# Three groups of 128-token chunks in place of four groups of mixed size, in a fused scan, MoE and Mish-MoE kernel

## The chip, the cores and the metric

The program runs on one core of a Trainium2 chip. The core has five engines with a queue of instructions each: TensorE (PE, matrix multiplies), VectorE (DVE), ScalarE (ACT), GpSimd (POOL) and SyncE (SP); POOL and SP are used here to issue DMAs. Every engine works its queue off in order and waits on semaphores for the others. The metric is the device time of one execution in microseconds (us); lower is better.

## The reference, cut to what matters

Three layers run one after the other on 4 sequences of 768 tokens, 8 heads of 48 (3072 tokens of 384):

```
mag = sqrt(a_re² + a_im²);  a = (a_re, a_im) · min(mag, 0.999) / (mag + 1e-6)
for t in range(768):                       # a complex, diagonal decay
    S = a[t] · S + k[t] v[t]ᵀ              # S is 48 x 48, complex, per head
    y[t] = q[t] · Re(S)
x  = ((y @ w1) * (y @ w2)) @ w3 @ w_out    # first MoE layer, 384 -> 1024 -> 384
h  = x @ w_in                              # second, 384 -> 2048 -> 384
out = (h * tanh(softplus(h))) @ w_out2
```

All values are float32.

## The kernel before, in words

The recurrence is cut into **chunks** of tokens. Inside a chunk the decays are multiplied up from the chunk's middle in both directions, so that scores inside the chunk become a masked matrix product, and between chunks a state `z` is carried. `GROUPS` (L24) lists half chunk lengths: a group holds 8 chunks of twice that length, in token order, and its tables are made together. `[32, 32, 64, 64]` is 16 chunks of 64 tokens, then 16 of 128.

Five kinds of work are written as Python generators ("streams") that yield a weight after each piece:

- `fold_stream` (F): decodes w3 and w_out and multiplies them together (matmuls into `ps_f`, halves `woh` and `wol`).
- `bh_stream(g)`, the **scan** of group g: for all chunks of a group at once, half length + 1 steps, in blocks of 7 steps (`BLK`). `norm` scales the decays of a block (L211 to L237, DVE and ACT in turn); `steps` makes three DVE instructions for each step (L261 `t`, L262 `rv`, L263 `p`), then two wide ones per block (L273 `kt`), which are written to DRAM (`kq_d`) through POOL from one buffer. The last block ends with the group's table `mt`; its last instruction is L299. A group of 32 has 33 steps in 5 blocks, one of 64 has 65 in 10.
- `ch_stream` (CH), the **chunks**: each loads its `tm` from `kq_d`, is transposed on PE (`ps_tr` L372), gives a state update (`ps_u` L380), scores (`ps_a` L415, masked on DVE in two halves, L416) and outputs (`ps_y` L428 and L433); the state goes on through L385, a DMA `ws<-w`, L403 and L404. A chunk can start only when its group's table is there. Its outputs go to DRAM (`xd`); when 512 tokens are there, they come back as one tile of the next layer (`xl`).
- `m1_all` (M), the first MoE layer: 6 tiles of 512 tokens of 8 **M1 steps** each. A step is 27 matmuls (`pa`, `pb`, `acc`, all at L500), with L519 on ACT and `u` L522 on DVE between. Tile 0 also decodes w1 and w2.
- `win_stream`: decodes the weights of the last layer.

`_merge` (L50) draws from several streams so that each advances in proportion to its weight; a stream that yields None waits for another. `until(CH, n)` stops after n chunks, `take(M, w)` after w units of M1 (a step is 6 units). What the merge writes is then ordered once more by the framework's scheduler on each engine, within what dependences allow; the engines' own order is what runs. After the streams, the last layer (`ps_h`, `ps_o`) runs with PE as good as always busy.

Chunks and M1 steps are counted from 0 below; "first table" is the `mt` of group 0, and so on.

Of the kernel before, what the change touches and what calls it, by code (L numbers as in the profile page):

```python
# [20 lines left out]
NT = B * S  # L21
NC = 8

GROUPS = [32, 32, 64, 64]  # L24
TOK0 = [2 * NC * sum(GROUPS[:g]) for g in range(len(GROUPS) + 1)]
assert TOK0[-1] == NT
CMAX = 2 * max(GROUPS)
SIZES = sorted({2 * l for l in GROUPS})
DFF1, DFF2 = 1024, 2048
# [20 lines left out]
def _merge(*gens):  # L50
    live = [[0.0, i, g, w] for i, (g, w) in enumerate(gens)]
    while live:
        live.sort(key=lambda s: (s[0], s[1]))
        s = live[0]
        try:
            w = next(s[2])
            if w is None and len(live) == 1:
                return
            s[0] = live[1][0] + 1e-3 if w is None else s[0] + w / s[3]
        except StopIteration:  # L60
            live.pop(0)
# [3 lines left out]
def kernel(  # L65
# [23 lines left out]
    mul, add, sub = ALU.mult, ALU.add, ALU.subtract  # L89
    NG = len(GROUPS)  # L90

# [5 lines left out]
    sg = const.tile([128, 1], F32, name="sg")  # L97
    n_blk = [-(-(l + 1) // BLK) for l in GROUPS]
    flags = const.tile([128, sum(n_blk) + 1], F32, name="flags")
    wsum = const.tile([128, 64], F32, name="wsum")  # L100
    cb = const.tile([128, 3], F32, name="cb")
    fss = [const.tile([64, 2, D], F32, name=f"fs{z}") for z in range(2)]
    kq_d = [dram.tile([128, l, 2 * D2], F32, name=f"kq_d{g}") for g, l in enumerate(GROUPS)]
    xd = [dram.tile([HD, TT], F32, name=f"xd{i}") for i in range(NTILE)]
# [53 lines left out]
    def fold_stream():  # L158

        wos, *bufs = [wpo.tile([128, 8 * HD], I32, tag=n, name="f" + n) for n in WN]  # L160
        bufs = [(w[:, 0:2048].rearrange("p (n z) -> p n z", z=2), w[:, 2048:3072]) for w in bufs]
        for c in range(3):
            decode(wo[:, c], 1024, wos[:, c * 1024:(c + 1) * 1024], bufs[c][0])
            yield 2.0
        wos = wos.bitcast(F32).rearrange("p (k n) -> p k n", k=8)
        for j in range(8):
            raw, dst = bufs[j % 3]
            f = decode(w3t[:, j], 1024, dst, raw).rearrange("p (k m) -> p k m", k=8)
            ps = mm_p.tile([128, HD], F32, tag="mm", name="ps_f")
            for kk in range(8):  # L170
                T.matmul(ps, lhsT=f[:, kk], rhs=wos[:, kk], start=(kk == 0), stop=(kk == 7))  # L171
            split(ps, woh[:, j], wol[:, j])
            for z, w in enumerate((woh, wol)):
                nc.sync.dma_start(out=w3o_d[:, z, j], in_=w[:, j].bitcast(F32))
            yield 2.0
        for n in WN:
            wt[n] = wpo.tile([128, 8, 3, 128], F32R, tag=n, name=n)
# [370 lines left out]
    def m1_all():  # L548
        for i in range(NTILE):
            while i not in done:  # L550
                yield None
            yield from m1_stream(i)

    def until(gen, n):
        for w in gen:
            yield w
            if chunks_done[0] >= n:
                return

    def take(gen, n):  # L560
        used = 0.0
        for w in gen:
            yield w
            used += w or 0.0
            if used >= n:
                return
# [13 lines left out]
    F = fold_stream()  # L580
    CH = ch_stream()
    M = m1_all()
    _merge((F, 22.0), (bh_stream(0), 54.0))
    _merge((until(CH, 8), 40.0), (bh_stream(1), 54.0), (take(M, 20.0), 30.0))
    _merge((until(CH, 16), 40.0), (bh_stream(2), 106.0), (take(M, 70.0), 70.0))
    _merge((until(CH, 24), 59.0), (bh_stream(3), 106.0), (take(M, 97.0), 97.0))
    bhs.close()
    fin_s = ExitStack()
    fa = fin_s.enter_context(tc.tile_pool(name="fa", bufs=1, side="right"))
# [352 lines left out]
```

## Time and profile before

| | |
|---|---|
| median of 3 runs | 1134.01 us (1128.3 to 1135.51) |
| the profiled execution: its own time | 1126.27 us |
| its span | 1124.5 us, mean granted clock 0.917 |
| busy over the span: PE | 1012.6 us (90%) |
| DVE, ACT, POOL | 701.5 (62%), 698.8 (62%), 110.2 us (10%) |
| the chain that ended last | PE 70%, ACT 13%, DVE 8%, DMA 5%, issue 3% |

Busy shares over the whole span hide that the stages differ. The tables of the groups are good marks, since the scans are the one work that cannot overlap itself: between them the profile's views by windows give a balance for each stage. A granted clock of 1.00 is 2.4 GHz on TensorE, 0.50 is 1.2 GHz.

### The profile page before, as it was taken

What the parts mean: (1) busy time and instruction counts of PE and PEld (TensorE: products, weight loads), DVE (VectorE), ACT (ScalarE), POOL (GpSimd) and SP (SyncE); (2) the same over time, 40 slices, a digit from 0 to 9 for tenths busy, and PEclk for the clock granted to TensorE, in tenths of its full rate; (3) what the DMA queues carried; (4) which work ended last, traced back from release to release, by engine and by line L of the source; (5) the groups of instructions that cost most, each with busy time, mean ns of one, the idle gap of its engine ahead of it and who ended that gap; (6) DMA issues with size and microseconds to landing.
All of it is one profiled execution on the core that took longest, in us unless ns stands there. A gap on an engine that the chain in (4) does not pass through costs nothing.

```text
span 1124.5 us, 15578 instructions
## 1 busy us (share of the span) xinstructions
PE 1012.6 (90%) x5594; PEld 814.7 (72%) x5594; DVE 701.5 (62%) x1564; ACT 698.8 (62%) x1308; POOL 110.2 (10%) x163
## 2 busy tenths in 40 slices
PE   0575999998669999999999999999999999999997
PEld 0343887676457887877888888877888888887876
DVE  4789787898969998336233532388565445555452
ACT  6875765887657665357444641699665645666572
POOL 1124131212222231100000000000000000000000
PEclk9897555898659999999999999999999999999999
DMA  7777575756669676446443320241010101000000
GB/s 273 235 222 214 146 183 147 215 161 177 173 174 226 161 205 162 95 129 172 113 107 90 120 85 1 64 119 43 10 47 1 57 1 57 1 0 29 1 29 31
DMA packets 77318, 125.77 MB, mean 112 GB/s; under 512 B 14648, under 2 KB 50576, under 8 KB 75824
## 3 DMA queue, kind: packets, MB, share of 16 engines
q1 hardware_dynamic: 65616, 86.63, 27.9%
q0 software_dynamic: 11616, 38.06, 12.4%
q8 instruction: 46, 0.75, 0.3%
q14 instruction: 40, 0.33, 0.1%
HBM read 84.25 MB, written 36.18 MB: 107 GB/s over the span
## 4 chain that ended last, share of the span: by engine, by line
PE 70%; ACT 13%; DVE 8%; DMA 5%; issue 3%; SPq 0%; POOL 0%; DVEq 0%; ACTq 0%; POOLq 0%
PE ps_o L500 15%; PE ps_h L500 13%; PE pa L500 8%; PE pb L500 8%; PE acc L500 8%; PE ps_u L380 4%; PE ps_a L415 4%; PE ps_tr L372 4%; PE ps_y L433 3%; PE ps_y L428 3%; ACT raw L151 2%; PE ps_f L171 1%; DMA ws<-w 1%; ACT dec L146 1%; ACT wb L638 1%
## 5 line engine op out<-in xcount | busy, mean ns | idle before, releaser
L500 PE MATMUL ps_o<-gh,wuh 128*128 128x512 f32 x288 | 112.6, 397 | 6.5 <-ACT gh L130 4.5
L500 PE MATMUL ps_o<-gl,wuh 128*128 128x512 f32 x288 | 113.1, 393 | 0.4 <-DVE gl L131 0.4
L500 PE MATMUL ps_h<-x2h,wih 128*128 128x512 f32 x288 | 113.3, 393 | 0.0
L500 PE MATMUL ps_h<-x2h,wil 128*128 128x512 f32 x288 | 113.2, 393 | 0.0
L500 PE MATMUL ps_o<-gh,wul 128*128 128x512 f32 x288 | 112.8, 392 | 0.0
L500 PE MATMUL ps_h<-x2l,wih 128*128 128x512 f32 x288 | 112.0, 389 | 0.0
L131 DVE TENSOR_TENSOR gl<-hb,gh 128x1024 fp32r<-128x1024 f32 x48 | 58.6, 1223 | 75.7 <-ACT gh L130 75.7
L638 ACT ACTIVATE wb<-ps_h 128x512 f32<-128x512 f32 x96 | 56.9, 605 | 71.2 <-PE ps_h L500 71.1
L639 DVE COPY hb<-ps_h 128x512 f32<-128x512 f32 x96 | 64.7, 687 | 47.6 <-ACT wb L638 45.5
L372 PE MATMUL ps_tr<-id_sb,tm 64*96 64x64 f32 (+1 forms) x512 | 67.0, 286 | 24.3 <-DMA tm<-kq_d 16.3
L522 DVE TENSOR_TENSOR u<-u,pb 128x512 f32<-128x512 f32 x48 | 32.9, 685 | 88.4 <-PE pb L500 78.2
L372 PEld LDWEIGHTS ps_tr<-id_sb,tm 64*96 64x96 f32 (+1 forms) x512 | 54.8, 152 | 36.7 <-issue 19.3
L130 ACT CAST gh<-hb 128x1024 fp32r<-128x1024 f32 x48 | 50.4, 1052 | 34.7 <-PE ps_o L500 34.7
L396 ACT ACTIVATE z<-w,tb 96x48 f32<-96x48 f32 x224 | 54.2, 321 | 26.1 <-DVE w L385 26.0
L500 PEld LDWEIGHTS ps_o<-gh,wuh 128*128 128x128 f32 x288 | 53.7, 188 | 22.7 <-ACT gh L130 6.6
L261 DVE TENSOR_TENSOR t<-an,p 128x192 f32<-128x192 f32 x192 | 67.7, 352 | 0.3
L500 PE MATMUL pa<-xh,w1h 128*128 128x512 f32 x144 | 60.8, 422 | 7.0 <-ACT xh L130 3.6
L519 ACT COPY u<-pa 128x512 f32<-128x512 f32 x48 | 28.2, 587 | 58.2 <-PE pa L500 57.9
L415 PE MATMUL ps_a<-qf,kf 96*64 96x64 f32 (+1 forms) x512 | 62.6, 288 | 1.9 <-ACT qf L373 1.9
L415 PEld LDWEIGHTS ps_a<-qf,kf 96*64 96x64 f32 (+1 forms) x512 | 59.0, 200 | 6.4 <-ACT qf L373 2.5
L500 PE MATMUL acc<-uh,woh 128*128 128x512 f32 x144 | 58.4, 418 | 5.5 <-ACT uh L130 5.5
L500 PEld LDWEIGHTS ps_h<-x2l,wih 128*128 128x128 f32 x288 | 54.1, 188 | 12.4
(157 smaller groups left out, 2490.0 us busy)
## 6 DMA issues: line engine op xcount, KB each, us to landing
tm<-kq_d SPq DMA_DIRECT2D x32, 384.0 KB, 5.3
an<-in_a POOLq DMA_DIRECT2D x26, 336.0 KB, 5.0
kqt<-in_kq POOLq DMA_DIRECT2D x26, 336.0 KB, 5.4
kq_d<-kt POOLq DMA_DIRECT2D x52, 168.0 KB, 4.4
kq_d<-kt POOLq DMA_DIRECT2D x26, 336.0 KB, 4.3
raw<-in_w SPq DMA_DIRECT2D x16, 384.0 KB, 4.8
tm<-kq_d SPq DMA_DIRECT2D x32, 192.0 KB, 4.0
raw<-in_win SPq DMA_DIRECT2D x16, 384.0 KB, 3.6
```

The costliest lines, as they stand in the source:

```text
L130: A.copy(out=hi, in_=raw)
L131: V.tensor_tensor(out=lo, in0=raw, in1=hi.bitcast(F32), op=sub)
L261: V.tensor_tensor(out=t, in0=win2, in1=_bc(pv[:, ::-1], 2, 2), op=mul)
L372: T.transpose(ps[:, hh], tm[n][:, h0 + hh, z], id_sb[0:C, 0:C])
L380: T.matmul(ps[:, h], lhsT=tm[n][:, h, 0], rhs=vt[n][:, h, 0:D], start=True, stop=True)
L396: A.activation(out=z[:, h, 0:D], in_=w[:, h], func=AF.Copy, scale=tbs[g][:, 0, c * H + h:c * H + h + 1])
L415: T.matmul(ps[:, hh], lhsT=kf[n][:, h], rhs=qf[n][:, h], start=True, stop=True)
L428: T.matmul(ps[DP * z:DP * z + DP, p], lhsT=st["z"][:, h], rhs=qf[n][:, h], start=True, stop=False)
L433: T.matmul(ps[DP * z:DP * z + DP, p], lhsT=vt[n][:, h], rhs=am[:, h], start=not inter, stop=True)
L500: T.matmul(ps, lhsT=l, rhs=r, start=first and n == 0, stop=final and n == len(seq) - 1)
L638: A.activation(out=wb[:, f % GRP], in_=ps, func=AF.Sigmoid, scale=-1.0)
L639: V.tensor_copy(hb[:, f % 2], ps)
```

## The change

Three groups of half length 64: 24 chunks of 128 tokens, three scans of 65 steps. The merge has one call less, and the weights of those that stay are those of a long scan and of large chunks.

```
-GROUPS = [32, 32, 64, 64]
+GROUPS = [64, 64, 64]
...
-    _merge((F, 22.0), (bh_stream(0), 54.0))
-    _merge((until(CH, 8), 40.0), (bh_stream(1), 54.0), (take(M, 20.0), 30.0))
-    _merge((until(CH, 16), 40.0), (bh_stream(2), 106.0), (take(M, 70.0), 70.0))
-    _merge((until(CH, 24), 59.0), (bh_stream(3), 106.0), (take(M, 97.0), 97.0))
+    _merge((F, 44.0), (bh_stream(0), 106.0))
+    _merge((until(CH, 8), 59.0), (bh_stream(1), 106.0), (take(M, 90.0), 90.0))
+    _merge((until(CH, 16), 59.0), (bh_stream(2), 106.0), (take(M, 90.0), 90.0))
```

The buffers, their numbers, the last two merges and the last layer are as they were. Three places show how instructions move.

DVE, from the last half of the folded weight (`wol`) on. Before, the group's last `kt` and its table follow at once:

```order
L131 TENSOR_TENSOR wol<-ps_f,woh 128x384
L273 TENSOR_TENSOR kt<-kqt,p 128x4x96 x2
L230 SCALAR_TENSOR_TENSOR an<-an,sg,sq 128x7x48
L294 TENSOR_TENSOR x_583<-p,fs_66 64x96
L295 TENSOR_TENSOR x_583<-p,fs_66 64x96
L296 TENSOR_TENSOR mt<-x_583 64x48
```

In the change the same instruction is followed by more of the scan of group 0:

```order
L131 TENSOR_TENSOR wol<-ps_f,woh 128x384
L261 TENSOR_TENSOR t<-an,p 128x192
L262 TENSOR_TENSOR rv<-rv 128x48
L263 TENSOR_TENSOR p<-t 128x96
L269 TENSOR_TENSOR kqt<-kqt,rv 128x7x48
L261 TENSOR_TENSOR t<-an,p 128x192
L211 TENSOR_TENSOR m_623<-sq 128x336
```

After this `wol` 34 of the group's 64 L261 are still to come ahead of the table; before, none was. Nothing of the fold stands among them.

PE, behind the first table (`ps_mt`) and one chunk. Before:

```order
L352 MATMUL ps_mt<-id_sb,mt 96x64 x2
L372 MATMUL ps_tr<-id_sb,tm 96x64 x16
L380 MATMUL ps_u<-vv,tm 96x48 x8
L415 MATMUL ps_a<-qf,kf 64x64 x8
L433 MATMUL ps_y<-am,vv 64x64 x4
```

In the change:

```order
L352 MATMUL ps_mt<-id_sb,mt 96x64 x2
L372 MATMUL ps_tr<-id_sb,tm 96x128 x16
L380 MATMUL ps_u<-vv,tm 96x48 x8
L415 MATMUL ps_a<-qf,kf 128x128 x8
L433 MATMUL ps_y<-am,vv 64x128 x4
```

A chunk has as many instructions as before, on twice the columns. Before, eight chunks stand here ahead of the first `pa`; in the change four and most of a fifth.

PE, one of the last eight chunks. Before, each of them has M1 work between its parts, as here in chunk 27:

```order
L372 MATMUL ps_tr<-id_sb,tm 96x128 x8
L380 MATMUL ps_u<-vv,tm 96x48 x8
L500 MATMUL acc<-uh,woh 128x512
L500 MATMUL acc<-ul,woh 128x512
```

In the change chunks 18 to 20 and the outputs of chunk 17 stand without any, as here chunk 19:

```order
L372 MATMUL ps_tr<-id_sb,tm 96x128 x12
L380 MATMUL ps_u<-vv,tm 96x48 x8
L415 MATMUL ps_a<-qf,kf 128x128 x8
L428 MATMUL ps_y<-qf,z_111 64x128 x2
L433 MATMUL ps_y<-am,vv 64x128 x2
L428 MATMUL ps_y<-qf,z_111 64x128 x2
```

The same holds of chunks 9 to 11 and of the outputs of chunk 8. Ahead of chunk 8 the change has some seven M1 steps with no chunk work between them.

## Rows read from the trace of the kernel before

**Rows 1.** The line of the table's last instruction: duration in ns, first and last start.
```profile
L299 DVE TENSOR_TENSOR mt<-x x4: 193/193/194, 98.6 to 452.6; 64x48 f32<-64x48 f32 x4
```

**Rows 2.** Windows, cut at three of the tables: stretch, length, busy us (instructions) by engine.
```profile
core 0: us, PE busy (x) PEld busy (x) DVE busy (x) ACT busy (x) POOL busy (x), PEclk, DMA share, GB/s
0.00:98.80 98.80, 48.44 (x129) 26.68 (x129) 72.18 (x208) 71.66 (x111) 21.91 (x35) 0.95 0.74 234
98.80:183.90 85.10, 72.98 (x595) 63.96 (x595) 70.57 (x234) 53.95 (x164) 21.69 (x32) 0.50 0.68 175
183.90:452.70 268.80, 236.64 (x1591) 189.81 (x1592) 235.75 (x712) 182.63 (x460) 65.01 (x94) 0.84 0.69 182
452.70:1124.00 671.30, 654.49 (x3288) 534.21 (x3282) 323.01 (x413) 390.57 (x573) 1.62 (x3) 1.00 0.21 58
```

**Rows 3.** Groups on DVE by shape, 0 to 700 us: busy us, mean ns; idle before.
```profile
L273 DVE TENSOR_TENSOR kt<-kqt,p 128x672 f32<-128x672 f32 x52 | 42.8, 849 | 0.0
L416 DVE TENSOR_TENSOR am<-ps_a,msk 128x512 f32<-128x512 f32 x32 | 22.0, 687 | 16.3 <-PE ps_a L415 15.9
L404 DVE TENSOR_TENSOR z<-z,ws 96x384 f32<-96x384 f32 x28 | 15.3, 548 | 0.6 <-ACT z L396 0.3
L416 DVE TENSOR_TENSOR am<-ps_a,msk 64x256 f32<-64x256 f32 x32 | 13.2, 414 | 15.1 <-PE ps_a L415 15.1
```

**Rows 4.** Timeline of DVE, one scan step and what follows: start, length in us.
```profile
404.60 0.35 DVE L261 TENSOR_TENSOR t<-an,p 128x192 f32<-128x192 f32 x1
404.87 0.20 DVE L262 TENSOR_TENSOR rv<-rv 128x48 f32<-128x48 f32 x1
404.99 0.26 DVE L263 TENSOR_TENSOR p<-t 128x96 f32<-128x96 f32 x1
405.17 0.50 DVE L217 TENSOR_TENSOR sq<-m,sq 128x336 f32<-128x336 f32 x1
405.58 0.35 DVE L261 TENSOR_TENSOR t<-an,p 128x192 f32<-128x192 f32 x1
```

**Rows 5.** The tile `kt`: its DMA issues on POOL (min/median/max ns), and their landing.
```profile
L277 POOL DMA_DIRECT2D kq_d<-kt x60: 527/736/773, 38.0 to 456.9; - x60
L275 POOL DMA_DIRECT2D kq_d<-kt x30: 532/568/586, 38.7 to 456.4; - x30
...
DMA to landing us min/median/max: 1.7/4.4/8.1
```

**Rows 6.** Timeline of PE, the start of a 64-token chunk and of the next.
```profile
125.81 1.94 PE L372 MATMUL ps_tr<-id_sb,tm 64*96 64x64 f32 x16
...
135.19 0.44 PE L372 MATMUL ps_tr<-id_sb,tm 64*96 64x64 f32 x2
```

**Rows 7.** Timeline of PE, the first 128-token chunk, and the next one's start.
```profile
338.64 3.29 PE L372 MATMUL ps_tr<-id_sb,tm 128*96 128x128 f32 x16 [8.11 <-DMA tm<-kq_d]
341.76 1.48 PE L380 MATMUL ps_u<-vv,tm 128*96 128x48 f32 x16
343.08 2.02 PE L415 MATMUL ps_a<-qf,kf 96*128 96x128 f32 x16
345.02 0.44 PE L428 MATMUL ps_y<-qf,z 96*64 96x128 f32 x4
...
346.93 0.53 PE L372 MATMUL ps_tr<-id_sb,tm 128*96 128x128 f32 x3
```

**Rows 8.** Windows inside that chunk's first part, columns as in rows 2.
```profile
341.00:342.00 1.00, 1.00 (x10) 0.97 (x8) 1.00 (x6) 1.00 (x4) 1.00 (x3) 0.78 1.03 237
```

**Rows 9.** Timeline of PE: half of a chunk's scores, just after a stall of PE.
```profile
531.21 1.71 PE L415 MATMUL ps_a<-qf,kf 96*128 96x128 f32 x8
```

**Rows 10.** Timeline of DVE: `u` of the last two M1 steps.
```profile
700.16 0.69 DVE L522 TENSOR_TENSOR u<-u,pb 128x512 f32<-128x512 f32 x1 [4.05 <-PE pb L500]
...
706.28 0.69 DVE L522 TENSOR_TENSOR u<-u,pb 128x512 f32<-128x512 f32 x1 [4.05 <-PE pb L500]
```

**Rows 11.** DMA issues of the large chunks' loads: count, KB each, median us to landing.
```profile
tm<-kq_d SPq DMA_DIRECT2D x32, 384.0 KB, 5.3
```

## The prediction, made before the changed kernel was timed

> **What bounds the kernel now.** The slices and busy shares of the page say PE at 90%, but they are a mean over stages, so I cut the trace at the tables first. The line of a table's last instruction runs four times, first at 98.6 us and last at 452.6 [rows 1]; a table is also where chunks of a new size become possible. The windows between the tables [rows 2] then show four different kernels:
> - To 98.8 us, fold and first scan: PE 48 of 98.8 us busy, DVE 72, ACT 72. DVE and ACT work in turn.
> - 98.8 to 183.9: the second short scan beside 64-token chunks, no M1 yet. PE 73 of 85 us busy, but at a granted clock of 0.50. A chunk comes each 135.19 - 125.81 = 9.4 us [rows 6], back to back: PE bounds, at 1.2 GHz.
> - 183.9 to 452.7: the two long scans, chunks and M1. DVE 235.75 of 268.8 us (88%), PE 236.64 (88%): both nearly full, DVE as the one that carries the scan.
> - From 452.7 on: PE 97% busy (654.49 of 671.3) at 1.00. Here only PE's work counts.
>
> **What the change does to each stretch.** I counted the instructions on DVE and PE between tables in the order of both programs. The result carries the whole sum:
>
> 1. *Third to last table against first to last.* Before, from the second to the fourth table, DVE does 128 scan steps with 19 block preambles, 19 M1 steps and 32 chunk halves (20 of 64 tokens, 12 of 128). In the change, from the first to the third table, it does 128 steps, 19 preambles, 19 M1 steps and 28 halves, all of 128. So these are the same stretch with other chunks.
> 2. *After the last table.* Both have 29 M1 steps, 10 chunks of 128 tokens and the last layer left on PE and DVE: equal work.
> 3. *What is left over.* The stretch of 85.1 us [rows 2] (32 steps of scan and the small chunks 0 to 6) is gone as a stretch of its own. Its scan is now the second half of group 0's, ahead of the first table and with the fold already done.
>
> So the time is 1126.27 - 85.1 + (the longer opening) + (differences in 1 and 2).
>
> **The longer opening, +48.** 32 more steps and 5 more blocks on DVE. A step is 0.27 (`t` to `rv`) + 0.12 (`rv` to `p`) + 0.18 (`p` to the next) = 0.57 us by starts; a 0.50 us instruction of the preamble takes 0.41 until the next starts [rows 4], since records overlap by about 0.08. So 32 x 0.57 = 18; 5 blocks x 8 instructions x 0.42 = 17; 8 more wide `kt` at 0.849 - 0.08 [rows 3] = 6; one pair of weight decodes moved ahead of the table, 2: together 43 us. That is the lower bound. DVE waits for ACT inside a preamble; between tables it reached 88% [rows 2], and in the change's order two steps stand between the dependent instructions of a preamble to cover ACT. I take 43/0.89 = 48. Upper bound: `kt` has one buffer, which comes free when POOL has issued three DMAs (0.57 + 2 x 0.74) and the last has landed (4.4, at most 8.1) [rows 5]; with 1.6 for its two instructions a block then takes 8.1 to 11.8 us. At 8.1 that is hidden in a block's 9; at 11.8 the opening is 5 x 11.8 = 59. PE idles through all of it, so it counts in full.
>
> **The middle stretch, +4.** In DVE time the chunk halves are 28 x 0.61 = 17 against 20 x 0.33 + 12 x 0.61 = 14 [rows 3]; state instructions (L385, L403, L404, 0.47 each) are 33 against 42, 4 us less; four more wide `kt` are 3 and two more decodes 1.5. Sum about +4 on 268.8, so 273. PE, in the same stretch: 14 chunks and 19 M1 steps. A step takes 706.28 - 700.16 = 6.1 us [rows 10]. A 128-token chunk took 346.93 - 338.64 = 8.3 us, of which the 3.1 of the transposes were at the low clock [rows 7]; at the high one that half falls away, 6.7. 14 x 6.7 + 19 x 6.1 = 210 us, less than the 237 now: DVE stays the bound. Bounds: at 92% of DVE's time 260; the high end is rival A below. Loads: each chunk still has two `tm` DMAs and one for `vv` on SP, of twice the bytes where chunks were small, landing in 5.3 us [rows 11] and prefetched by a chunk or two; SP issues a quarter fewer in all. The scans' DMAs on POOL are as many blocks as before. The first chunk's load waits for the scan's last write, before as now (8.11 us of PE idle at such a place [rows 7]), and DVE goes on with the next scan under it.
>
> **The end, +10.** Work is equal, but before all of the last eight chunks have M1 between their parts; now three and a half stand alone, while M1 has run ahead. Alone, PE waits for ACT's copies and DVE's masks: 8.3 against 6.7 is 1.6 a chunk, 6 us, and the tile that chunk 19 completes has its way through DRAM with one chunk to cover it, some 4 more. Bounds: 0, and 3.5 x (12.9 - 6.7) = 22, all at the low clock (rival B).
>
> Sum: 1126.27 - 85.1 + 48 + 4 + 10 = 1103 us, 2.1% less. The profiled execution is 0.7% below the median of the runs shown; in terms of that median 1103 x 1134.01/1126.27 = **1110 us**.
>
> **The clock, where row and rule part.** 64-token chunks ran for 85 us at 0.50 with PE 86% busy [rows 2]; the first 128-token chunk, also alone and after 8 us of idleness, had its clock raised within 3 us of its first transpose (0.78 in the microsecond in which it rose [rows 8]). I take that the large chunks get 2.4 GHz where they follow each other. The Trainium skill, "TensorE: Matmul & The Clock Gate", Part 1, says that the throttled state is the default and that busy time releases it: by that rule the small chunks should have been released too, and rival B would have next to no chance, with 1110 as the sum; by the rows B keeps one. The measured stretch decides.
>
> **Rivals.**
> - *A: lock step in the middle; slower.* Ahead of chunk 8 the change has seven M1 steps in a row on PE, beside a scan: 6.1 us of PE each and, by the order, about as much on DVE, where each step's `u` and low half stand behind pieces of scan. PE has two buffers for `pa` and `pb`, so it can't run far ahead. If the two engines then take turns, a step takes up to 12.3 us: for the eight steps of that tile +46, so 1149 (1157 in terms of the median). It decides from 9 us a step. Against it: both were 88% busy at once in the old middle stretch [rows 2]. For it: no chunk fills the gaps now. 12%.
> - *B: chunks alone at 1.2 GHz.* Large chunks, when they wait for DVE, may be at the low clock as the small ones were: 3.1 for transposes, 2.6 (twice 1.32) and 3.4 (2 x 1.7 [rows 9]) for update and scores, 3.8 (2 x 1.91) for outputs, 12.9 us. Eight such in the middle: 8 x 12.9 + 6 x 6.7 + 116 = 259 us of PE, at 88% 295 instead of 273; at the end 22 instead of 10. Together +34: 1137 (1145), slower by 0.9%. It decides from 10.5 us a chunk, since up to there DVE is the slower one. 18%.
> - *C: better.* The opening near its floor (44), DVE at 92% in the middle, chunks alone without stalls: 1126.27 - 85.1 + 44 - 9 + 1 = 1077 (1085). 12%.
> - That the change does nothing can be left out: the order has 24 chunks and one scan less.
>
> **Chances and range.** My forecast, 1090 to 1120 in terms of the median, has 58%. The range reaches over C and most of B: 1085 to 1150; A is left out with part of B. About 1% is what a measurement of this kernel tells from no change. Faster by more: the forecast and C but for the edge, 67%; within 1%: the better half of B and that edge, 17%; slower: A and the other part of B, 16%.
>
> **What would show it.** The first table at 140 to 160 us, with PE idle for about 50 us ahead of it; the last table at 405 to 435 instead of 452.7; PE's busy time down by some 40 to 80 us; a granted clock near 1.00 in the transposes of the chunks that stand alone. Wrong would be: an opening over 60; M1 steps over 9 us ahead of chunk 8; chunks 9 to 11 or 18 to 20 over 11 us each.

## The result

| | before | after |
|---|---|---|
| median | 1132.51 us (4 runs, 1128.3 to 1135.51) | 1102.55 us (4 runs, 1101.78 to 1105.23) |
| ratio | | 0.9742, 95% interval 0.9704 to 0.978 |
| the profiled execution: time, span | 1126.27, 1124.5 us | 1102.09, 1100.3 us |
| PE busy, PE idle in the span | 1012.6, 111.9 us | 936.0, 164.3 us |

The change makes the kernel 2.6% faster. (The median of before has one run more than in the prediction; the forecast of 1110 was made against 1134.01.)

**Where the time went.** First the tables and the windows between them, as in [rows 1, 2]; the row 98.00:143.80 is the part of the opening in which the scan is alone.

```profile
L299 DVE TENSOR_TENSOR mt<-x x3: 194/194/194, 143.8 to 424.5; 64x48 f32<-64x48 f32 x3
```

```profile
core 0: us, PE busy (x) PEld busy (x) DVE busy (x) ACT busy (x) POOL busy (x), PEclk, DMA share, GB/s
0.00:143.80 143.80, 51.12 (x128) 28.31 (x128) 114.42 (x356) 96.55 (x167) 35.63 (x54) 0.79 0.67 205
98.00:143.80 45.80, 0.00 (x0) 0.00 (x0) 45.56 (x165) 23.97 (x57) 17.11 (x25) 0.52 0.52 143
143.80:424.50 280.70, 228.36 (x1548) 191.78 (x1549) 247.50 (x748) 193.60 (x464) 72.02 (x105) 0.90 0.77 201
424.50:1100.00 675.50, 656.54 (x3277) 536.46 (x3275) 324.95 (x413) 390.40 (x572) 1.62 (x3) 0.99 0.20 57
```

The stretch of 85.1 us is gone, the opening is 143.8 instead of 98.6, the middle 280.7 instead of 268.8, the end 675.8 instead of 671.8: -85.1 + 45.2 + 11.9 + 4.0 = -24.0, which is the difference of the spans but for rounding. The same difference on PE reads another way. Its busy time fell by 76.6 us, and its idle time grew by 52.4: by 42 ahead of the first table (143.8 - 51.12 against 98.8 - 48.44), by 8 from there to the last, by 2 behind it. Eight chunks fewer pay for a longer idle stretch at the start.

PE's waits from the first table to the last (and for the table itself) name what grew. The loads of the chunks cost 28.5 us of waiting, against 16.3 in the kernel before, and the way of finished tiles through DRAM (`xh`) 9.1 against 2.0.

```profile
engine line waited for: us in total, times, longest us
PE ps_mt L352 <- DVE mt L297: 46.8, 1, 46.8
PE ps_tr L372 <- DMA tm<-kq_d: 28.5, 3, 19.3
PE pa L500 <- ACT xh L130: 9.1, 2, 5.4
```

In the timeline of PE the first chunk waits 19.3 us (8.1 at the place in [rows 7]) and takes 3.62 us for its sixteen transposes; two chunks later the same sixteen take 1.96. The granted clock was 0.76 from 164 to 172 us and 1.00 from 172 to 182. The two later chunks that wait for a load, 3.7 and 5.5 us, take 3.49 and 3.62 us again. The chunks that stand alone and don't wait for a load start 7 to 8 us apart (the one at 357.70 is followed by the next at 365.26), the last three 6.8 us (536.11 to 549.67 is two of them).

```profile
163.66 3.62 PE L372 MATMUL ps_tr<-id_sb,tm 128*96 128x128 f32 x16 [19.30 <-DMA tm<-kq_d]
...
180.80 1.96 PE L372 MATMUL ps_tr<-id_sb,tm 128*96 128x128 f32 x16
...
357.70 1.96 PE L372 MATMUL ps_tr<-id_sb,tm 128*96 128x128 f32 x16
...
386.16 3.62 PE L372 MATMUL ps_tr<-id_sb,tm 128*96 128x128 f32 x16 [5.50 <-DMA tm<-kq_d]
...
536.11 2.01 PE L372 MATMUL ps_tr<-id_sb,tm 128*96 128x128 f32 x16
...
549.67 2.01 PE L372 MATMUL ps_tr<-id_sb,tm 128*96 128x128 f32 x16
```

### The profile page after: what moved, and what is told of

It is laid out like the page before. It is cut to its first block, busy times and chain, and to the rows that moved or that the text cites. A ratio compares the mean times of both kernels' runs of the same rounds, so it can differ in the third digit from the quotient of the medians.

```text
span 1100.3 us, 14021 instructions
## 1 busy us (share of the span) xinstructions
PE 936.0 (85%) x4952; PEld 756.6 (69%) x4952; DVE 686.9 (62%) x1513; ACT 680.6 (62%) x1203; POOL 109.3 (10%) x161
## 4 chain that ended last, share of the span: by engine, by line
PE 59%; ACT 15%; DVE 11%; DMA 10%; issue 5%; POOL 0%; SPq 0%; DVEq 0%; ACTq 0%; POOLq 0%
PE ps_o L500 16%; PE ps_h L500 13%; PE pa L500 6%; PE pb L500 6%; PE acc L500 5%; DMA xl<-xd 3%; PE ps_f L171 3%; PE ps_tr L372 2%; DMA xd<-ysb 2%; PE ps_a L415 2%; ACT raw L151 2%; DVE t L261 2%; PE ps_y L433 2%; DVE kt L273 1%; DMA an<-in_a 1%
## 5 line engine op out<-in xcount | busy, mean ns | idle before, releaser
L372 PE MATMUL ps_tr<-id_sb,tm 128*96 128x128 f32 x384 | 58.7, 305 | 30.2 <-DMA tm<-kq_d 28.5
L372 PEld LDWEIGHTS ps_tr<-id_sb,tm 128*96 128x96 f32 x384 | 48.0, 141 | 39.3 <-issue 32.7
L500 PE MATMUL pa<-xh,w1h 128*128 128x512 f32 x144 | 60.2, 418 | 15.8 <-ACT xh L130 13.6
L261 DVE TENSOR_TENSOR t<-an,p 128x192 f32<-128x192 f32 x192 | 67.9, 354 | 1.4 <-ACT an L232 1.3
L130 ACT CAST uh<-u 128x512 fp32r<-128x512 f32 x48 | 29.9, 623 | 58.8 <-DVE u L522 58.6
L500 PEld LDWEIGHTS ps_o<-gl,wuh 128*128 128x128 f32 x288 | 54.1, 188 | 12.5 <-DVE gl L131 0.8
L500 PEld LDWEIGHTS ps_h<-x2h,wil 128*128 128x128 f32 x288 | 54.0, 188 | 12.5
L500 PEld LDWEIGHTS ps_o<-gh,wul 128*128 128x128 f32 x288 | 54.1, 188 | 12.0
```

Of the source, the lines that this page charges most:

```text
L130: A.copy(out=hi, in_=raw)
L261: V.tensor_tensor(out=t, in0=win2, in1=_bc(pv[:, ::-1], 2, 2), op=mul)
L372: T.transpose(ps[:, hh], tm[n][:, h0 + hh, z], id_sb[0:C, 0:C])
L500: T.matmul(ps, lhsT=l, rhs=r, start=first and n == 0, stop=final and n == len(seq) - 1)
```

## The experiments

Twelve kernels, each against the kernel before on its own chip; the change itself has 0.9742 (0.9704 to 0.978). Table times, end, PE busy and idle are of one profiled execution each (the change: 143.8, 424.5, 675.8, 936, 164).

| run | ratio, interval | first, last table | end | PE busy, idle |
|---|---|---|---|---|
| e1 small chunks, new order | 1.0151 (1.0107 to 1.0195) | 100.6, 460.8 | 681.6 | 1012, 131 |
| e2 fold spread | 0.9772 (0.9731 to 0.9814) | 145.3, 429.5 | 673.7 | 942, 161 |
| e3 last kt apart | 0.9852 (0.9812 to 0.9891) | 143.5, 437.8 | 670.6 | 945, 163 |
| e4 M1 late | 1.0013 (0.9989 to 1.0037) | 143.1, 424.7 | 706.1 | 950, 181 |
| e5 small chunks last | 1.0365 (1.0333 to 1.0398) | 143.9, 465.9 | 703.3 | 1000, 169 |
| e6 layout | 0.975 (0.9708 to 0.9792) | 142.3, 420.1 | 673.7 | 934, 160 |
| e7 layout, fold spread | 0.9779 (0.9744 to 0.9815) | 145.1, 425.6 | 673.7 | 944, 155 |
| e8 layout in before | 1.0005 (0.998 to 1.003) | 100.8, 454.6 | 673.3 | 1013, 115 |
| e9 half of kt on ACT | 0.9727 (0.9684 to 0.977) | 148.8, 407.9 | 691.7 | 937, 162 |
| e10 leaner M1 | 0.9619 (0.958 to 0.9657) | 144.2, 440.4 | 644.1 | 892, 193 |
| e11 half of kt on POOL | 0.9889 (0.9849 to 0.9929) | 145.9, 417.6 | 697.7 | 938, 177 |
| e12 chunks ahead | 0.9736 (0.9698 to 0.9773) | 143.7, 443.4 | 656.5 | 942, 158 |

### Order or chunk size: e1, e5

e1 keeps the small chunks and takes the order:

```
-    _merge((until(CH, 8), 40.0), (bh_stream(1), 54.0), (take(M, 20.0), 30.0))
-    _merge((until(CH, 16), 40.0), (bh_stream(2), 106.0), (take(M, 70.0), 70.0))
-    _merge((until(CH, 24), 59.0), (bh_stream(3), 106.0), (take(M, 97.0), 97.0))
+    _drain(bh_stream(1))
+    _merge((until(CH, 16), 80.0), (bh_stream(2), 106.0), (take(M, 90.0), 90.0))
+    _merge((until(CH, 24), 59.0), (bh_stream(3), 106.0), (take(M, 90.0), 90.0))
```

> The groups of the kernel before (32, 32, 64, 64), but with the order of the change: the second scan alone right after the first, no chunk beside it, then the chunks beside the two long scans with M1 drawn by 90 in both. This parts the two things that the change does at once, the order and the chunk size. Theory 'the order pays' (the 85 us stretch was long because scan 1 was interleaved with lone 64-token chunks in lock step): the second scan alone takes 40 to 46 us instead of 85.1, so the second table stands near 140; the sixteen small chunks then cost DVE about 11 us more than eight large ones, so the last table near 436 and the whole at about 1110 to 1118. Rival 'the chunk size pays' (small chunks hold PE at 1.2 GHz and cost it 9.4 us per 64 tokens wherever they stand): PE needs 16 x 9.4 + 6 x 6.7 + 19 x 6.1 = 307 us between the second and the last table, more than DVE's 258, so the last table near 475 and the whole at 1135 to 1155, no faster than before.

It took 1145.91 us, 1.5% more than before, as the rival said, though the last table came at 460.8 and not near 475. The first two windows of e1 reach from the second table to the last, the third is its second scan:

```profile
150.20:283.40 133.20, 110.91 (x822) 90.56 (x823) 111.48 (x351) 83.79 (x240) 36.79 (x54) 0.59 0.66 174
283.40:460.80 177.40, 169.94 (x1164) 136.31 (x1164) 140.77 (x406) 120.65 (x302) 32.44 (x48) 0.91 0.67 172
100.60:150.20 49.60, 14.87 (x114) 13.57 (x114) 49.15 (x185) 30.67 (x77) 18.15 (x27) 0.52 0.70 188
```

Without chunks in its way the second scan took 49.6 us with DVE 99% busy, not 85.1, so the old stretch was held up by its chunks. But the chunks moved to the next stretch took the time there: 310.6 us from the second table to the last against 268.8 before, at clocks of 0.59 and 0.91, and PE's busy time stayed at 1012. So this order, with small chunks, saves nothing.

e5 has large chunks first and cuts the change's last group in two:

```
-GROUPS = [64, 64, 64]
+GROUPS = [64, 64, 32, 32]
...
-    _merge((until(CH, 16), 59.0), (bh_stream(2), 106.0), (take(M, 90.0), 90.0))
+    _merge((until(CH, 12), 30.0), (bh_stream(2), 54.0), (take(M, 45.0), 45.0))
+    _merge((until(CH, 16), 30.0), (bh_stream(3), 54.0), (take(M, 45.0), 45.0))
```

> The change with its last group cut in two (64, 64, 32, 32): the last 1024 tokens are sixteen 64-token chunks, which stand beside M1 here, and at the end, instead of alone at the front. The first scan and the opening stay as in the change. Theory 'small chunks are dear because alone they run at 1.2 GHz': beside M1 they get 2.4 GHz, cost PE half of 9.4 us each, 16 x 4.7 = 75 instead of 8 x 6.7 = 54, so the total is 1118 to 1130 and PE's busy time 955 to 965. Rival 'small chunks take the clock down wherever they stand': 16 x 9.4 = 150 us, PE busy above 1000, total 1150 to 1200. Rival 'their number does not matter where M1 covers them': within 8 us of the change, 1095 to 1110.

It took 1170.65 us with PE 1000 us busy: the time that the first rival named, but only in part for its reason. Windows cut to one tile (PE's busy time and count first) show e5's small chunks beside M1 at a granted clock of 1.00, where PE was 99% busy; the tiles are `ps_tr`, `ps_u`, `ps_a`, `ps_y`:

```profile
477.00:565.00 88.00, 8.86 (x108) 6.82 (x108) 9.00 (x27) 1.00 0.23 64
477.00:565.00 88.00, 9.18 (x96) 8.60 (x96) 2.77 (x5) 0.48 (x1) 1.00 0.23 64
477.00:565.00 88.00, 7.93 (x96) 6.41 (x96) 4.99 (x12) 1.00 0.23 64
477.00:565.00 88.00, 12.47 (x176) 8.74 (x176) 2.24 (x6) 1.00 0.23 64
```

and the same four of the change, large chunks beside M1:

```profile
440.00:545.00 105.00, 10.63 (x80) 8.62 (x80) 10.22 (x20) 1.00 0.40 109
440.00:545.00 105.00, 5.18 (x55) 5.20 (x55) 1.10 (x2) 0.47 (x1) 1.00 0.40 109
440.00:545.00 105.00, 8.29 (x64) 7.92 (x64) 5.52 (x8) 1.00 0.40 109
440.00:545.00 105.00, 8.79 (x128) 6.89 (x128) 2.92 (x5) 1.00 0.40 109
```

Per record that is 82, 96, 83 and 71 ns for small chunks, 133, 94, 130 and 69 for large ones. A chunk has 16, 16, 16 and 32 of them, so a small chunk costs PE some 6.4 us and a large one 7.9, at the same clock, for twice the tokens. (The records overlap a little: from one start to the next, lone large chunks took 6.8 us.) Sixteen small ones in place of eight large ones are 16 x 6.4 - 8 x 7.9 = 39 us of PE at 2.4 GHz, and at the 9.4 us of [rows 6] 87. The 76.6 us that the change saved lie between, since before only part of the small chunks ran at 0.50. So by this estimate about half of what the small chunks cost PE is their number, and about half the clock.

The clock's half shows in e5 too. From 577 to 603 us no M1 stands between its small chunks. With PE 99% busy on both sides of 577 us the granted clock fell from 1.00 (565 to 577) to 0.55 (577 to 582), and in the stretch below it was 0.50:

```profile
585.00:603.00 18.00, 17.83 (x151) 15.48 (x149) 9.15 (x20) 13.94 (x38) 0.00 (x0) 0.50 0.68 180
```

e5 has 64 us more of PE's busy time than the change, 39 of them by this count; that the other 25 are such stretches was not measured one by one.

### Opening: e2

```
-    _merge((F, 44.0), (bh_stream(0), 106.0))
+    _merge((F, 22.0), (bh_stream(0), 106.0))
```

> The change with the fold's weight halved (22 instead of 44), so that the fold is spread over the whole first scan instead of its first half. In the change DVE is 70% busy up to 98 us (68.9 of 98) and 99% from there to the first table (45.56 of 45.8). Theory 'the opening is bound by DVE where the scan is alone, by the turns of DVE and ACT where the fold is': mixed evenly, the 114.4 us of DVE fill 88 to 95% and the first table comes at 120 to 130 instead of 143.8; everything after it moves along, total 1078 to 1090. Rival 'the fold's pace is set by its own chain of loads, ACT and DVE, and the scan beside it by its own': the shares do not rise, the table stays at 140 to 148, total 1098 to 1106.

As the rival said, the first table came at 145.3 us and the total is that of the change. PE's wait for the table is 16 us instead of 47, but its wait ahead of the fold grew from 34.7 to 51.1 us; chunk 0 starts at 155.4, yet nothing is gained. The opening of e2 in three windows:

```profile
0.00:50.00 50.00, 0.00 (x0) 0.00 (x0) 30.71 (x95) 40.12 (x63) 11.30 (x19) 1.00 0.67 227
50.00:100.00 50.00, 33.99 (x78) 18.51 (x79) 47.13 (x142) 35.46 (x60) 13.60 (x20) 0.83 0.75 244
100.00:145.30 45.30, 21.65 (x51) 11.45 (x49) 42.07 (x146) 24.30 (x52) 15.13 (x24) 0.74 0.55 154
```

In the first 50 us DVE is busy for 30.7 us, in the change for 30.1: that slack, 8.1 us of it one wait for ACT, the spread doesn't touch. From there on DVE is 94% busy, with 119.9 us in all ahead of the table, 5.5 more than in the change, since five steps of the next scan moved ahead of it. So what the spread filled it filled with later work, and behind 50 us DVE sets the opening.

### Loads: e3, e6, e7, e8

e3 gives a scan's last, one-row `kt` a buffer of its own:

```
-                kt = bh.tile([128, m, 2, 2, D], F32, tag="kt", name="kt", bufs=1, padded_shape=[128, BLK, 2, 2, D])
+                kt = bh.tile(
+                    [128, m, 2, 2, D], F32, tag="kt" if m > 1 else "kt1", name="kt", bufs=1,
+                    padded_shape=[128, BLK if m > 1 else 1, 2, 2, D],
+                )
```

> The change with a buffer of its own for the last, one-row kt of a scan. In the change that kt stands 10.4 us behind the one ahead of it (141.37 to 151.79), since both share one buffer, and chunk 0's transposes wait until 163.66, 19.3 us after the table's transpose. Theory 'the one buffer of kt makes the wait': the last kt is written ahead of the table, the load of chunk 0 is issued 4 to 9 us earlier, its transposes start at 150 to 159; since DVE goes on with the next scan meanwhile and paces this stretch, the total falls by only 0 to 5 us (1097 to 1102). Rival 'the load waits for DMA engines that are 92% busy': the transposes still start at 160 or later, total within 2 us of the change.

The rival had the cause: the loads were issued at 148.91 instead of 154.59, 5.7 us earlier, and chunk 0 still started only at 162.1, 1.6 us earlier. Issues between 143 and 164 us (columns: tile, queue, count, size, median us to landing), of e3:

```profile
tm<-kq_d SPq DMA_DIRECT2D x4, 384.0 KB, 12.2
an<-in_a POOLq DMA_DIRECT2D x2, 336.0 KB, 8.8
```

and of the change:

```profile
tm<-kq_d SPq DMA_DIRECT2D x4, 384.0 KB, 8.7
an<-in_a POOLq DMA_DIRECT2D x2, 336.0 KB, 6.3
```

The load issued earlier took longer to land, and so did the scan's own (`an`) beside it. The last table came 13 us later and the total is about 1% above the change, which neither theory had. Between the tables DVE's busy time stayed (247.15 us) and its waits grew: for PE's scores 8.7 us instead of 1.6, for PE's state updates 5.0 instead of 1.0, for ACT's part of one `an` 4.4 instead of 1.3. Why they grew is open.

e6 changes the layout of `kq_d`, so that `tm` is read in 6 KB pieces instead of 768 B ones; e8 is the same in the kernel before.

```
-    kq_d = [dram.tile([128, l, 2 * D2], F32, name=f"kq_d{g}") for g, l in enumerate(GROUPS)]
+    kq_d = [dram.tile([2, l, NC * H, 2 * D2], F32, name=f"kq_d{g}") for g, l in enumerate(GROUPS)]
...
-                        out=kq_d[g][64:128, s0:s0 + m, (1 - z) * D2:(2 - z) * D2],
+                        out=kq_d[g][1, s0:s0 + m, :, (1 - z) * D2:(2 - z) * D2].rearrange("s p d -> p s d"),
...
-            src = kq_d[g].rearrange("(a c h) s d -> a c s h d", a=2, c=NC)
+            src = kq_d[g].rearrange("a s (c h) d -> a c s (h d)", c=NC)
```

> The change with kq_d laid out by step first (2, l, 64 heads and chunks, 192), so that the load of tm reads 6 KB pieces instead of 768 B ones, while the write of kt's first half falls from whole rows to 768 B pieces; bytes and dependences are the same. In the change the DMA engines are 92% busy from 143.8 to 200 us and chunk 0 waits 19.3 us for its load; with the last kt written earlier the load was issued 5.7 us sooner and landed only 1.6 us sooner. Theory 'the small pieces of the loads fill the DMA engines, and that is what the middle stretch lost against my sum': landing of tm falls from 5.9 to 3 to 4.5 us, chunk 0 starts at 152 to 159 instead of 163.7, the middle stretch is 268 to 276 instead of 280.7, total 1090 to 1098. Rival 'the writes of kt and the other loads fill them': landing stays over 5 us, total 1099 to 1106. Rival 'DVE paces the middle whatever the loads do': landing falls, the total stays within 3 us of 1102.

> The same layout with the fold spread over the whole first scan (weight 22). The spread alone started chunk 0 at 155.4 instead of 163.7, but left the first table (145.3) and the total as they were. Theory 'what the spread saves is lost to loads behind it': with both, chunk 0 starts at 150 to 154 and the total is 3 to 8 us below the layout alone. Rival 'the scan paces': same as the layout alone within 3 us.

> The layout in the kernel before. There the small chunks are bound by PE at 1.2 GHz (86% busy) and the DMA share is 0.68 to 0.69. Theory 'the loads cost the change more than they cost the kernel before, so part of its gain was lost to them': the kernel before gains 0 to 3 us, less than the change does with the layout. Rival 'the loads cost both alike': the kernel before gains as much as the change, 5 us or more.

In e6, between 143 and 300 us, the median landing of `tm` went from 7.1 to 6.3 us, the packets of that stretch from 23080 to 14238, the middle from 280.7 to 277.8, and the ratio is that of the change. e7 doesn't differ from it, and e8 gains nothing. So the theory of e6 fails: what fills the DMA engines there is more than the small pieces of this load. Which of its two rivals holds stays open, since the landing stayed over 5 us, as the first said, and DVE's busy time between the tables stayed too (247.72 us), as the second would have it; 1098.22 us lies just below the range of either. e8 can't tell its theories apart, since the change gained nothing measurable either.

### What sets the middle: e4, e9, e10, e12

e4 draws less M1 in the two middle merges, e12 draws the chunks faster there; e9 and e10 take work off one engine. Both compute less: e9 leaves out the multiplication by `p` in half of `kt`, e10 two products of three in tiles 0 and 1.

```
e4
-    _merge((until(CH, 8), 59.0), (bh_stream(1), 106.0), (take(M, 90.0), 90.0))
-    _merge((until(CH, 16), 59.0), (bh_stream(2), 106.0), (take(M, 90.0), 90.0))
+    _merge((until(CH, 8), 59.0), (bh_stream(1), 106.0), (take(M, 18.0), 18.0))
+    _merge((until(CH, 16), 59.0), (bh_stream(2), 106.0), (take(M, 30.0), 30.0))
e12
+    _merge((until(CH, 8), 100.0), (bh_stream(1), 106.0), (take(M, 90.0), 90.0))
+    _merge((until(CH, 16), 100.0), (bh_stream(2), 106.0), (take(M, 90.0), 90.0))
e9
-                    V.tensor_tensor(out=kt[:, :, z], in0=_bc(kqt[:, :, z], 2, 2), in1=p[:, 0:m], op=mul)
+                V.tensor_tensor(out=kt[:, :, 0], in0=_bc(kqt[:, :, 0], 2, 2), in1=p[:, 0:m], op=mul)
+                A.copy(out=kt[:, :, 1], in_=_bc(kqt[:, :, 1], 2, 2))
e10
-            seq += [(lh, rh), (lh, rl), (ll, rh)]
+            seq += [(lh, rh)] if lean else [(lh, rh), (lh, rl), (ll, rh)]
```

In e10 `lean` is true for tiles 0 and 1.

> The change with M1 drawn by 18 and 30 instead of 90 and 90 in the two middle merges: 10 M1 steps stand ahead of the last table on DVE instead of 19, so nine go behind it. Theory 'ahead of the last table DVE paces and PE's work is nearly free, behind it only PE's work counts': DVE is relieved of 9 x 1.3 = 12 us, so the last table comes at 405 to 415 instead of 424.5, and the end grows by 9 x 6.1 = 55 us; total 1138 to 1150. Rival 'M1 in the middle holds the scan up by its PE time': the middle shortens by up to 9 x 6.1 us, last table at 370 to 385, total 1100 to 1110.

> The change with DVE relieved: the second of the two wide kt products of every block is a plain copy on ACT (the multiplication by p is left out for that half, so its values are not the reference's). That takes 0.85 us a block off DVE, some 8 us ahead of the first table and 15 between the first and the last, and two M1 steps move behind the last table. Theory 'DVE paces the opening and the middle', on which my sum rests: first table at 134 to 137 instead of 143.8, middle 262 to 270 instead of 280.7, end 676 + 2 x 6.1 = 688; total 1084 to 1095. Rival 'the turns between DVE, ACT and the chunks pace them, and relief of DVE turns into waits' (nine M1 steps fewer left the table where it was): first table at 141 to 145, middle 277 to 285, total 1106 to 1118.

> The change with PE relieved in the middle: M1 of tiles 0 and 1 uses one product of three (9 matmuls a step instead of 27; the two correction products of these tiles are left out). That takes 16 x 4.1 = 65 us of PE work away ahead of the last table, none behind it, and by the order three more M1 steps come ahead of the table. Theory 'PE has slack in the middle': the last table moves by less than 8 us from 424.5, the end shortens by the three steps, 676 - 18 = 658, total 1075 to 1090. Rival 'M1 and scan in lock step': the middle falls by 25 to 65 us, last table at 360 to 400, total 1020 to 1060.

> The change with the chunks drawn faster (weight 100 instead of 59) in the two middle merges: by the order sixteen chunks and twenty M1 steps have their DVE parts ahead of the last table instead of fourteen and nineteen. The runs so far say that DVE sets when the last table comes and that behind it the time is PE's work. Theory 'work brought ahead of the last table saves its PE time at the end and costs its DVE time in the middle': DVE gets 2 x 2.6 for the chunks and 1.3 for the step, so the last table comes near 431 instead of 424.5; PE is spared 2 x 7 + 6.1 = 20 us behind it, so the end is near 656 instead of 675.8; total 1085 to 1093, better than the change. Rival 'chunks without M1 beside them stall DVE in its order': the last table comes 15 us or more later, total 1100 or more.

Middle and end, as windows, of e4, e9, e10 and e12 in turn:

```profile
143.10:424.70 281.60, 211.36 (x1478) 172.44 (x1478) 239.72 (x739) 187.25 (x462) 71.99 (x105) 0.84 0.77 203
424.70:1130.50 705.80, 690.29 (x3347) 564.76 (x3346) 331.67 (x422) 395.51 (x574) 1.63 (x3) 1.00 0.19 54
```

```profile
148.80:407.90 259.10, 220.19 (x1443) 185.55 (x1444) 216.70 (x676) 190.31 (x450) 69.18 (x101) 0.89 0.78 203
407.90:1099.30 691.40, 670.14 (x3383) 547.46 (x3381) 330.45 (x422) 394.69 (x586) 1.37 (x3) 0.99 0.21 57
```

```profile
144.20:440.40 296.20, 216.70 (x1484) 175.97 (x1486) 255.53 (x763) 200.77 (x489) 71.93 (x105) 0.81 0.73 194
440.40:1084.20 643.80, 622.90 (x3058) 508.00 (x3052) 315.67 (x399) 380.77 (x549) 1.63 (x3) 0.99 0.20 58
```

```profile
143.70:443.40 299.70, 253.65 (x1703) 215.93 (x1703) 255.19 (x759) 200.81 (x483) 71.97 (x105) 0.89 0.75 192
443.40:1099.60 656.20, 637.46 (x3122) 520.64 (x3121) 318.33 (x402) 383.13 (x553) 1.62 (x3) 0.99 0.20 57
```

Against the change (DVE 247.50 in the middle, PE 656.54 in the end):

| | DVE busy, middle | length, middle | PE busy, end | length, end |
|---|---|---|---|---|
| e4 | -7.8 | +0.9 | +33.8 | +30.3 |
| e9 | -30.8 | -21.6 | +13.6 | +15.9 |
| e10 | +8.0 | +15.5 | -33.6 | -31.7 |
| e12 | +7.7 | +19.0 | -19.1 | -19.3 |

The right half is one rule: behind the last table the length follows PE's work nearly one for one. The left half follows DVE in direction, but for e4, and not in size. e10 excludes PE's M1 work as what sets the middle: with M1 at a third of its matmuls on tiles 0 and 1 the last table came 16 us later, as three more steps and two more chunks stood ahead of it. e9 says DVE leads: 31 us less on it gave 22 back (7 steps of the next scan had moved ahead of the first table, which explains its 148.8). e4's theory was half wrong: nine steps went behind, but two chunks came forward in their place (PE's records behind grew by 70, not 243), so DVE was relieved by 8 us instead of 12, and waits on `w` (4.9 us instead of 0.6 up to the second table) and on ACT took that. e12 shows why the size differs: chunks without M1 beside them stall DVE. Its waits for PE's scores were 9.2 us instead of 1.6, for `ws` 9.7 instead of 6.2, for PE's state updates 3.9 instead of 1.0.

The totals of e9 and e12 teach most. e9 brought the last table forward by 16.6 us and its end grew by 15.9, since by its order two M1 steps and a chunk more stood behind; e12 did the reverse and lost what it won, its rival's case (table at 443.4). Neither beats the change beyond the intervals (0.9727 and 0.9736 against 0.9742), and e10, which does, computes less. In e2, e3, e6, e7, e9 and e12 PE's idle time is 155 to 163 us and the time 1098 to 1111: moving the table moved work across it. Why the idle time holds so well is open.

### Half of kt on POOL: e11

```
-                for z in range(2):
-                    V.tensor_tensor(out=kt[:, :, z], in0=_bc(kqt[:, :, z], 2, 2), in1=p[:, 0:m], op=mul)
+                for z, eng in ((1, nc.gpsimd), (0, V)):
+                    eng.tensor_tensor(out=kt[:, :, z], in0=_bc(kqt[:, :, z], 2, 2), in1=p[:, 0:m], op=mul)
```

> The change with the second wide kt product of every block on POOL instead of DVE, all values as in the reference: a version that could beat both kernels. POOL is 10% busy, but issues the scan's DMAs in order, so that its 128x672 product stands ahead of the block's kq_d writes. No row here shows arithmetic on POOL: at 0.85 us, as on DVE, the total would be that of the copy on ACT, 1084 to 1095 where DVE paces; at several times that, say 5 us, a block of 9 us would still cover it, and chunk 0 would start some 4 us later, total 1090 to 1105. Rival 'POOL and DVE hold each other up': DVE's steps take longer than 0.57 us beside it, total over 1105.

As the rival said, the total is over 1105: 1116.02 us. DVE's busy time rose from 686.9 to 700.2 with 27 of its wide products gone; the last section has the reason.

## Why the prediction came out right, and where its terms were off

1102.55 against 1110 forecast, inside the range; the sum in the profiled execution's terms was 1103 and it took 1102.09. Three errors of single terms, -2.8, +7.9 and -6.0 us, nearly cancelled: that the sum came out to 1 us is luck. The step from 1103 to 1110 was not borne out: the changed kernel's profiled execution lies at its median (1102.55), not 0.7% below it.

- **Opening, +45.2 (forecast 48, from 43 to 59): right.** The scan alone ran with DVE 45.56 of 45.8 us busy, so nearly at the floor; ACT was covered better than the 89% assumed, and the one `kt` buffer cost nothing inside the opening. Right behind it the buffer delays the last `kt`, which is written at 151.79, behind the table; by e3 a buffer of its own gains nothing.
- **Middle, +11.9 (forecast 4, from 260 to 295 in length): the term was mis-sized.** That "from the second to the fourth table, DVE does 128 scan steps with 19 block preambles" was counted in the order of the program. In the trace, of before:

```profile
L261 DVE TENSOR_TENSOR t<-an,p 128x192 f32<-128x192 f32 x122 | 43.0, 353 | 0.3
L211 DVE TENSOR_TENSOR m<-sq 128x336 f32<-128x336 f32 x16 | 8.0, 500 | 0.0
```

 and of after, between its tables:

```profile
L261 DVE TENSOR_TENSOR t<-an,p 128x192 f32<-128x192 f32 x128 | 45.3, 354 | 1.4 <-ACT an L232 1.3
L211 DVE TENSOR_TENSOR m<-sq 128x336 f32<-128x336 f32 x17 | 8.5, 499 | 0.1
```

 Six steps and a block's preamble, 6 x 0.57 + 8 x 0.42 = 6.8 us, had been done inside the 85.1 us that the sum took off whole. That is most of the 8 us. The state's instructions were also overrated: 36 of L385, L403 and L404 before, 33 after, so 1.6 us saved and not 4. DVE's busy time between the tables rose by 11.75 us and its idle time stayed at 33, so here the stretch grew by as much as DVE's work.
- **End, +4.0 (forecast 10, from 0 to 22): too dear.** The lone chunks 18 to 20 took 6.8 us each, not 8.3; PE idled 19.0 us there against 16.8.
- **Rival A** is excluded: the `u` of the eight M1 steps ahead of and in chunk 8 run from 297.3 to 343.4, 6.6 us a step, against 9 at which it would have decided; e10 excludes the lock step too.

```profile
297.33 0.69 DVE L522 TENSOR_TENSOR u<-u,pb 128x512 f32<-128x512 f32 x1
...
343.39 0.68 DVE L522 TENSOR_TENSOR u<-u,pb 128x512 f32<-128x512 f32 x1
```

- **Rival B** is excluded for the chunks that follow each other (6.8 to 8.2 us, its point was 10.5). The low clock showed behind the three waits for a load (19.3, 3.7 and 5.5 us), where the transposes took 1.5 to 1.7 us more.
- **That PE bounds the small chunks' stretch, at 1.2 GHz: right, but not for the clock alone.** e1 shows the 49.6 us that the scan needs, e5 that a small chunk is dear at 2.4 GHz as well and falls to 1.2 where it has no M1 beside it.
- **"DVE stays the bound" in the middle** holds in direction (e9, e10), but DVE's busy time alone does not give the length (e4, e12).
- **The first chunk's load**, put at the 8.11 us of PE's idle time of [rows 7], took 19.3. That cost the sum nothing that shows: in e2 it was 9.5, and the time the same.
- **What the prediction counted on without showing it**: that equal work stays behind the last table. It did here. e9 and e12 show that a sum over tables is worth nothing where it doesn't.

**The clock.** 128-token chunk 0, alone, began at the low clock (0.76 from 164 to 172 us) and chunk 2 ran at the high one (1.00); 64-token chunks had 0.50 at 86% busy for 85 us [rows 2], 0.50 at 99% for 18 us in e5 without M1, and 1.00 in e5 where M1 stood between them. "TensorE: Matmul & The Clock Gate", Part 1, of the Trainium skill says that busy time releases the throttle. The large chunks and e5's stretch with M1 agree with it; [rows 2] and e5's stretch without M1 don't, so the rows remain the better guide to a lone stretch of small matmuls.

## What to carry to other kernels

Count instructions before columns: at the same clock a chunk of 64 tokens took 6.4 us of TensorE and one of 128 took 7.9, so fewer, fuller pieces paid, and none of the reorderings tried here did. When stages hand over at marks such as these tables, read the work between two marks from the trace and not from the program, and check which work an edit moves across a mark: a scan that ends 17 us earlier was worth nothing when PE's work moved behind it. Issuing a load earlier need not bring it in earlier: here, with the DMA engines 92% busy (143.8 to 200 us), 5.7 us at the issue became 1.6 at the first use.

## What the runs showed of the hardware that was not expected

An elementwise product on POOL held up the DVE instruction beside it. In e11, POOL and then DVE at the same moment:

```profile
115.38 1.66 POOL L273 TENSOR_TENSOR kt<-kqt,p 128x672 f32<-128x672 f32 x1
```

```profile
115.08 0.50 DVE L221 SCALAR_TENSOR_TENSOR y<-sq,y 128x336 f32<-128x336 f32 x1
115.49 1.66 DVE L263 TENSOR_TENSOR p<-t 128x96 f32<-128x96 f32 x1
117.08 0.55 DVE L155 SCALAR_TENSOR_TENSOR dec<-dec,raw 128x384 int32<-128x384 int32 x1
```

A `p` that takes 0.25 us alone took 1.66 beside it. Beside 22 of the 27 wide products on POOL stands a DVE instruction of 1.5 us or more; beside the other five DVE was idle for most of the time or had `ps_a` or `pb` in PSUM as one input. Such a product saves DVE the 0.85 us of its own and here cost it 1.4, by the sum over all (13.3 us more in spite of 27 x 0.85 less). The Trainium skill, "SBUF — State Buffer", section "Who interferes with whom", says that a DVE instruction with two SBUF inputs contends with a GpSimd instruction that reads SBUF, and that the ports they share are an exclusive lock; this row agrees.

Eight times larger pieces (6 KB instead of 768 B) shortened a 384 KB load's landing by only 0.8 us, 7.1 to 6.3 in the median between 143 and 300 us (e6), where the DMA engines were 82% busy up to the second table in the change and 79% in e6.
